# Products and query tiles in column halves, with a new allowance for other work, in a fused long convolution and attention

## The chip, the cores and the metric

The kernel runs on one core of one Trainium2 chip. The metric is the device time of one execution in microseconds (us). All data is float32.

## What is computed

Two independent results stand side by side in the output. The first 576 columns are a long convolution: a kernel `K` of 2048 steps for each of 576 channels, made from a sum of 128 complex exponentials a channel, is convolved with `u`. The other 576 columns are attention with 32 query heads of 18 columns and one shared key and value head, over 2048 positions.

```python
P = jnp.exp(logdA[:, :, None] * l[None, None, :])
K = jnp.einsum("dn,dnl,dn->dl", Cc, P, dB).real
y = irfft2(rfft2(up) * rfft2(Kp))[:L] + u * Dskip

q = (x @ wq).reshape(B, S, H, Dh);  k = x @ wk;  v = x @ wv
p = softmax(einsum("bhqd,bkd->bhqk", q, k) * Dh ** -0.5)
out = einsum("bhqk,bkd->bhqd", p, v).reshape(B, S, H * Dh) @ wo
```

## The kernel before, in words

**The attention rounds.** `main` (line 664) walks over 1024 pairs in a fixed order: 4 chunks of 512 queries, 8 groups of four heads, 16 blocks of 128 keys, 2 pairs of heads. A pair has a score tile of 128 keys by 2 x 512 queries. The pairs are taken in rounds of three (`NS`). In a round TensorE (PE) makes the scores of three pairs (`scores`, line 419), ScalarE (ACT) takes their exponentials from PSUM into an SBUF tile `P` (`exponentials`, line 430), and PE multiplies earlier `P` tiles with V (`product`, line 721). One product covers two pairs, that is four heads: four matmuls in the four 32-column strips of the array, 512 columns wide, into the bank `ops`; it adds up over 16 key blocks. Then VectorE (DVE) copies `ops` out (`gather`, line 440) and the next group of heads may begin. PSUM has three score tiles of two banks, one bank for `ops`, and one bank `f` for all other work. There are eight `P` tiles (`NP`).

**Other work.** Three streams of other work are written as generators that yield before each piece: the query projections and output projections (`side`: `qproj`, line 322; `outproj`, `outproj_part`), the preparation of outputs (`prep`), and the convolution (`conv`). The convolution runs over 12 pieces of 48 channels: tables of exponentials on DVE, kernel tiles on PE (`kgen`), transforms on PE (`transform`, tiles `lu`, `hu`, `lk`, `hk`), products on DVE, inverse transforms on PE (`iy`), and a few long ACT functions (sine, exponential) with table loads. Every PE piece of other work writes the bank `f` and DVE must empty it before the next tile.

**What sets the order.** The instructions of PE, ACT and DVE are emitted in an order written by the program itself. A `Clock` in the program keeps planned times for the three engines (each piece adds a fixed charge: 0.88 a product, 0.465 a query group, 0.485 an output-projection group). Between scores and products, `fill` (line 690) hands out pieces of other work while an allowance (`credit`) or the planned time before the next scores permits it; the constants in lines 37 to 46 set it. `free` (line 765) is the planned time at which all three score buffers are free. Queues are in order: a piece that waits holds up what is behind it on its engine.

**Query tiles.** `qproj` makes a tile of 126 (or 72) rows by 512 queries in ten groups of four matmuls, 256 columns each, into one bank. DVE then makes three passes over all 512 columns from that bank: `qh` (a rounded copy), `ql` (the remainder), `ab` (the largest absolute value); the bank is free after the third. `queries` (line 359) stores `qh` and `ql` to DRAM, makes `aw` and a small bound matmul `up` from `ab`, and `fetch` reads the stored rows back into `aug`, from which the scores are made. `qh` and `ql` have one buffer each. The first query tile (`first_queries`, line 351) uses these two buffers as well.

**The end.** `outproj_part` adds the output projection of the last chunk in parts while the rounds still run; `finish` (line 535) does the parts that are left (`rest`) after the last products, scales the last group and stores.

Of the kernel before, what the change touches and what calls it, by code (L numbers as in the profile page):

```python
# [17 lines left out]
P = 128  # L18
# [17 lines left out]

RATE = 1.75
PACE = 1.68
AHEAD = 0.7
TOTAL = 340.0  # L40
LAST = 500
DEFER = 0.5
NAUG = 5
HEAD = 12

LEFT = 0.85

# [13 lines left out]
class Clock:  # L61
# [6 lines left out]
    def __init__(self):  # L68
        self.t = self.v = self.a = 0.0
        self.work = 0.0  # L70
        self.s = [0.0] * NS
        self.fill = 0.0

    def pe(self, cost, *after):
# [6 lines left out]
    def filled(self):  # L81

        self.fill = self.v + 0.25

    def dve(self, out, rate):
# [35 lines left out]
class Stream:  # L121
# [26 lines left out]
    def go(self, step, credit, lock=None):  # L148

        k = self.k  # L150
        ready = self.ready if self.kind != "p" or self.holds else max(self.ready, k.fill)
        if not self.live or self.kind == "b" or self.kind == "p" and (credit <= 0 or k.t < ready or lock not in (None, self)):
            return False
        if self.kind == "v" and (k.t < self.ready or k.v > k.t + self.ahead):
            return False
        if self.kind == "w":
            if self.asked == step:
                return False
            self.asked = step
        self.advance()  # L160
        return True
# [10 lines left out]
class Attention:  # L172
# [36 lines left out]
    def setup(self, tp, conv):  # L209
# [17 lines left out]

        keys = cp.tile([P, 5, CT], F32R, tag="oT", name="keys")
        kh, kl, self.vt = keys[:, 0, :], keys[:, 1, :], keys[:, 2, :].bitcast(F32)
        self.ident = cp.tile([P, P], F32, name="ident")  # L230
# [91 lines left out]
    def qproj(self, c, m, xt):  # L322

        nc, V, K = self.nc, self.V, self.k
        m0, mn = MT[m]
        self.q_left = 10
        yield "p", K.fill, False
        ps = self.bank(CT, f"q{c}_{m}")
        for f in range(2):
            sl = slice(f * 256, f * 256 + 256)  # L330
            for k in range(5):
                matmul4(nc, ps[:, sl], self.wq[m][:, k, :], xt[:, k, sl], start=(k == 0), stop=(k == 4))
                K.pe(0.465)
                self.q_left -= 1
                self.units += 1
                if (f, k) != (1, 4):
                    yield "p", 0.0, True
        K.v = max(K.v, K.t)
        qh, ql, ab = self.operands(c, m)
# [4 lines left out]
        yield from self.queries(c, m, qh, ql, ab)  # L344

    def operands(self, c, m):
        return (self.p2.tile([P, CT], F32R, tag="qh", name=f"qh{c}_{m}", bufs=1),
                self.p2.tile([P, CT], F32R, tag="ql", name=f"ql{c}_{m}", bufs=1),
                self.p2.tile([P, 2], F32, tag="ab", name=f"ab{c}_{m}"))

    def first_queries(self, ps):
        nc, V, mn = self.nc, self.V, MT[0][1]
        qh, ql, ab = self.operands(0, 0)
        nc.scalar.activation(qh[:mn, :], ps[:mn, :], AF.Copy)
        V.tensor_tensor(ql[:mn, :], ps[:mn, :], qh[:mn, :].bitcast(F32), op=ALU.subtract)
        V.tensor_reduce(ab[:mn, 0:1], ps[:mn, :], axis=AX.X, op=ALU.max, apply_absolute_value=True)
        yield from self.queries(0, 0, qh, ql, ab)

# [125 lines left out]
    def outproj(self, c):  # L484
# [4 lines left out]
        for t in range(4):  # L489
            ob = self.p1.tile([P, D], F32, tag="ob", name=f"ob{c}_{t}")  # L490
            for n in range(2):
                cs = slice(n * 288, (n + 1) * 288)
                ps = self.bank(288, f"op{c}_{t}_{n}")
                for m, (m0, mn) in enumerate(MT):
                    matmul4(nc, ps, o[:mn, m, t * P:(t + 1) * P], self.wo[:mn, m, cs], start=(m == 0), stop=(m == 4))
                    K.pe(0.485)
                    self.o_left -= 1
                    self.units += 1
                    if m < 4:
                        yield "p", 0.0, True  # L500
# [166 lines left out]
    def main(self, conv, flag):  # L667
# [22 lines left out]
        def fill(then):  # L690
# [3 lines left out]
            while more:  # L694
                more = False
                credit = state["credit"] - (K.t - t - idle)
                urgent = self.due < self.step + 8
                late = self.late()
                for st in (prep, side, conv) if urgent else (prep, conv, side):
# [18 lines left out]
            state["filled"] += K.t - t  # L718
            state["credit"] = max(state["credit"] - (K.t - t), -0.8)

        def product(n):
            nonlocal o_ps
            c, g, kb, _ = pairs[2 * n]
            if kb == 0:
                fill(self.o_free)
                o_ps = self.ps_o.tile([P, CT], F32, tag="o", name=f"ops{c}_{g}")
            for j in range(4):
                nc.tensor.matmul(o_ps[32 * j:32 * j + 32, :], self.v[:, kb, :], pts[2 * n + j // 2][:, j % 2, :],  # L728
                                 start=(kb == 0), stop=(kb == 15), tile_position=(0, 32 * j))
            K.pe(0.88, done[2 * n + 1] + 0.1, self.o_free if kb == 0 else 0.0)  # L730
            read[n] = K.t + 0.2
            state["credit"] -= 0.88
            if kb == 15 and (c, g) != (NCH - 1, 7):
# [6 lines left out]
        for r in range(0, len(pairs), NS):  # L740
# [12 lines left out]
            for i in new:  # L753

                while (i - NP) // 2 >= behind:
                    product(behind)
# [5 lines left out]

            state["credit"] = min(state["credit"] + NS / 2 * (0.88 + min(max((TOTAL - state["filled"]) / max(LAST - s, 20), 0.45), 0.7 if s < 384 else 0.9)), 1.2 + 0.88)
# [16 lines left out]
            if kb >= 12 and nxt < 64:  # L780
                force(lambda: nxt in self.ready)
        while behind < len(pairs) // 2:
            product(behind)
# [95 lines left out]
class Conv:  # L879
# [203 lines left out]
    def transform(self, src, y, nm, ready):  # L1083
# [4 lines left out]
        for j in range(2):  # L1088
            for half in (1, 0):
                yield "p", max(ready, K.fill), False  # L1090
                ps = self.bank(2 * NE, f"{'lh'[half]}{nm}{j}").rearrange("p (r n) -> p r n", r=2)
                for r in (2 * half, 2 * half + 1):
                    q = 4 * j + r
                    matmul4(nc, ps[:, r % 2, :], self.dft[:, q * P:(q + 1) * P], src(r))
                    K.pe(0.33)
                    if r % 2 == 0:
                        yield "p", 0.0, True
# [15 lines left out]
    def back(self, k, kt):  # L1113
# [58 lines left out]
        for hf in range(2):  # L1172
# [3 lines left out]
            for r in (2 * hf, 2 * hf + 1):  # L1176
                for j in range(2):
                    q = 8 + 4 * j + r
                    matmul4(nc, ps[:, r % 2, :], self.dft[:, q * P:(q + 1) * P], w[:, 4 * j + r, :], start=(j == 0), stop=(j == 1))
                K.pe(0.65)  # L1180
                if r % 2 == 0:
                    yield "p", 0.0, True
# [158 lines left out]
```

## Time and profile before

| | |
|---|---|
| median of 3 runs | 1245.04 us (1243.87 to 1247.54) |
| profiled execution | 1244.84 us |
| its span, first to last instruction | 1242.8 us |
| mean granted PE clock | 0.983 |
| first and last exponential start | 33.0 and 1220.5 us |
| PE, DVE, ACT busy | 1161.4, 987.5, 1048.6 us |

An engine's busy time counts each moment once in which it has an instruction in work; PE's is no measure of PE at its peak, since matmuls overlap. In a timeline row stand the start, the length, engine, line, operation, the tiles and, behind `x`, how many records were merged; in brackets the idle time before it and what ended it. A float32 matmul leaves two records, so a group of four matmuls is `x8`. PEld is PE's loading of weights, which runs beside PE. The chain of waits goes back from the last instruction to what released each step.

### The profile page before, as it was taken

What the parts mean: (1) busy time and instruction counts of PE and PEld (TensorE: products, weight loads), DVE (VectorE), ACT (ScalarE), POOL (GpSimd) and SP (SyncE); (2) the same over time, 40 slices, a digit from 0 to 9 for tenths busy, and PEclk for the clock granted to TensorE, in tenths of its full rate; (3) what the DMA queues carried; (4) which work ended last, traced back from release to release, by engine and by line L of the source; (5) the groups of instructions that cost most, each with busy time, mean ns of one, the idle gap of its engine ahead of it and who ended that gap; (6) DMA issues with size and microseconds to landing.
All of it is one profiled execution on the core that took longest, in us unless ns stands there. A gap on an engine that the chain in (4) does not pass through costs nothing.

```text
span 1242.8 us, 32583 instructions
## 1 busy us (share of the span) xinstructions
PE 1161.4 (93%) x13786; PEld 478.1 (38%) x13786; DVE 987.5 (79%) x1606; ACT 1048.6 (84%) x1101; POOL 53.6 (4%) x93
## 2 busy tenths in 40 slices
PE   7799999999999899899999899999998989999997
PEld 2344333334334334334334334334433334433433
DVE  4576986996897897796898895798589899799573
ACT  2598979899998888888988888888898988988893
POOL 2010000100000000000000000000000000000000
PEclk8799999999999999999999999999999999999999
DMA  6532222213223112023223002122212211111111
GB/s 228 163 98 80 82 61 67 74 37 111 77 86 106 34 36 83 25 72 103 95 53 116 28 20 72 56 76 79 80 35 62 88 34 63 42 49 61 60 40 41
DMA packets 55051, 89.32 MB, mean 72 GB/s; under 512 B 14173, under 2 KB 24797, under 8 KB 54388
## 3 DMA queue, kind: packets, MB, share of 16 engines
q1 hardware_dynamic: 43911, 72.46, 18.1%
q0 software_dynamic: 10016, 13.98, 4.4%
q8 instruction: 110, 1.80, 0.6%
q10 hardware_dynamic: 972, 0.74, 0.2%
q14 instruction: 42, 0.34, 0.1%
HBM read 49.28 MB, written 36.50 MB: 69 GB/s over the span
## 4 chain that ended last, share of the span: by engine, by line
PE 60%; DVE 27%; ACT 5%; issue 4%; DMA 2%; SPq 1%; ACTq 0%; DVEq 0%
PE ops L728 24%; PE s L426 16%; DVE tab L99 5%; PE op L169 5%; ACT P L437 4%; PE q L169 3%; DVE ks L99 3%; DVE acc L99 3%; PE kg L1051 3%; PE iy L169 2%; DVE pt L99 2%; DVE f L99 2%; DVE r L99 2%; PE lk L169 1%; PE hk L169 1%
## 5 line engine op out<-in xcount | busy, mean ns | idle before, releaser
L437 ACT ACTIVATE P<-s 128x1024 f32<-128x1024 f32 x992 | 937.7, 1031 | 134.6 <-PE s L426 130.2
L728 PE MATMUL ops<-P,v_sb 128*32 128x512 f32 x4096 | 519.7, 600 | 10.9 <-DVE o L103 10.8
L426 PE MATMUL s<-aug,kaug 55*128 55x512 f32 x2048 | 365.3, 443 | 28.8 <-ACT P L437 23.5
L426 PEld LDWEIGHTS s<-aug,kaug 55*128 55x128 f32 x2048 | 170.2, 185 | 343.2 <-ACT P L437 301.1
L728 PEld LDWEIGHTS ops<-P,v_sb 128*32 128x32 f32 x4096 | 115.6, 110 | 159.1 <-issue 115.7
L169 PE MATMUL q<-x,wq_sb 128*32 128x256 f32 (+2 forms) x1480 | 105.9, 397 | 2.7 <-DVE sck L99 1.2
L169 PE MATMUL op<-wo_sb,oT 126*32 126x288 f32 (+1 forms) x1088 | 83.4, 430 | 7.7 <-DVE sck L99 3.7
L169 PEld LDWEIGHTS q<-x,wq_sb 128*32 128x32 f32 (+1 forms) x1480 | 47.4, 110 | 54.3 <-issue 25.6
L99 DVE TENSOR_TENSOR tab<-tab,tt 128x576 f32<-128x576 f32 (+1 forms) x72 | 59.1, 821 | 1.6
L103 DVE COPY ksb<-kg 128x192 f32<-128x192 f32 x48 | 17.5, 364 | 53.7 <-PE kg L1051 53.6
L99 DVE TENSOR_TENSOR tab<-tab 128x576 f32<-128x576 f32 (+1 forms) x72 | 59.0, 819 | 1.1
L99 DVE TENSOR_TENSOR tab<-sum,r 128x576 f32<-128x576 f32 (+1 forms) x72 | 58.9, 818 | 0.0
L99 DVE TENSOR_TENSOR tt<-f,sum 128x576 f32<-128x576 f32 (+1 forms) x72 | 58.9, 817 | 0.0
L99 DVE TENSOR_TENSOR tab<-r,dif 128x576 f32<-128x576 f32 (+1 forms) x72 | 58.8, 816 | 0.0
L169 PEld LDWEIGHTS op<-wo_sb,oT 126*32 126x32 f32 (+1 forms) x1088 | 33.1, 114 | 51.8 <-issue 28.4
L435 ACT ACTIVATE P<-s,nb 128x1024 f32<-128x1024 f32 x32 | 33.1, 1115 | 22.8 <-PE s L426 22.6
L99 DVE TENSOR_TENSOR pt<-us,ks 128x1728 f32<-128x1728 f32 (+2 forms) x36 | 48.6, 1351 | 0.1
L99 DVE TENSOR_TENSOR acc<-acc,pt 128x1728 f32<-128x1728 f32 (+2 forms) x36 | 48.6, 1351 | 0.1
L99 DVE TENSOR_TENSOR sck<-lk,sck 128x384 f32<-128x384 f32 x48 | 24.5, 553 | 28.2 <-PE lk L169 28.2
L1051 PEld LDWEIGHTS kg<-tab 128*32 128x32 f32 x2304 | 36.7, 111 | 24.5 <-issue 8.8
L376 POOL DMA_DIRECT2D qd<-qh x38 | 24.0, 635 | 498.4 <-DVE qh L103 498.4
L1051 PE MATMUL kg<-tab 128*32 128x64 f32 x2304 | 42.4, 223 | 1.9 <-DVE tab L99 1.5
(131 smaller groups left out, 992.9 us busy)
## 6 DMA issues: line engine op xcount, KB each, us to landing
aug<-qd SPq DMA_DIRECT2D x124, 110.0 KB
od<-o SPq DMA_DIRECT2D x31, 256.0 KB
qd<-qh POOLq DMA_DIRECT2D x30, 252.0 KB, 6.0
u<-u SPq DMA_DIRECT2D x12, 384.0 KB
kd<-ksb SPq DMA_DIRECT2D x12, 384.0 KB
kt<-kd SPq DMA_DIRECT2D x48, 96.0 KB
outa<-u SPq DMA_DIRECT2D x12, 384.0 KB
oT<-od SPq DMA_DIRECT2D x16, 252.0 KB
```

What stands on the lines that cost most here:

```text
L99: return self.v.tensor_tensor(out, *a, **k)
L103: return self.v.tensor_copy(out, *a, **k)
L169: nc.tensor.matmul(ps[j:e], w[:, j:e], x, start=start, stop=stop, tile_position=(0, j))
L376: q.dma_start(qd[h0 + n0:h1, row:row + 18, :], src[n0 * DH:mn, :].bitcast(F32))
L426: nc.tensor.matmul(ps[:, j, :], self.kaug[r, kb * P:(kb + 1) * P], t[r, :], start=True, stop=True)
L435: nc.scalar.activation(pt, ps, AF.Exp, scale=SCALE, bias=self.nb)
L437: nc.scalar.activation(pt, ps, AF.Exp, scale=SCALE)
L728: nc.tensor.matmul(o_ps[32 * j:32 * j + 32, :], self.v[:, kb, :], pts[2 * n + j // 2][:, j % 2, :], start=(kb == 0), stop=(kb == 15), tile ...
L1051: nc.tensor.matmul(ps[32 * g:32 * g + 32, d, :], t[:, :32], t[:, 32:], start=(j == 0), stop=(j == 1), tile_position=(0, 32 * g))
```

## The change

- A product is made in two halves of 256 columns, each with its own four matmuls; the unit that the rounds hand out is the half, and a round's due is three halves. A half is charged 0.435 in the clock.
- A query tile is made in two halves of 256 columns, each in a tile of its own in the bank `f`. DVE copies each half and makes its remainder; then the bank counts as free; the maximum is taken from the copy in SBUF, by halves, and a third small reduction joins the two.
- The first query parts stand in two unused slices of the `keys` tile, not in the buffers of `qh` and `ql`.
- `fill` computes its allowance with new constants, and DVE's run ahead of the plan is cut by `NEAR` while a PE piece that needs emptying, or the end of a product sum, is planned soon (`near`, `due`, `last`).

```diff
-RATE = 1.75
-PACE = 1.68
-AHEAD = 0.7
-TOTAL = 340.0
-LAST = 500
-DEFER = 0.5
+RATE = 1.7223
+PACE = 2.6661
+AHEAD = 0.6441
+TOTAL = 238.4006
+LAST = 660.2161
+DEFER = 0.3799
...
+    def near(self):
+        return NEAR if self.t + SOON > min(self.due, self.last) else 0.0
...
-        if self.kind == "v" and (k.t < self.ready or k.v > k.t + self.ahead):
+        if self.kind == "v" and (k.t < self.ready or k.v > k.t + self.ahead - k.near()):
...
+        qh, ql, ab = self.operands(c, m)
         for f in range(2):
             sl = slice(f * 256, f * 256 + 256)
+            yield "p", K.fill, False
+            ps = self.bank(256, f"q{c}_{m}_{f}")
             for k in range(5):
-                matmul4(nc, ps[:, sl], self.wq[m][:, k, :], xt[:, k, sl], start=(k == 0), stop=(k == 4))
+                matmul4(nc, ps, self.wq[m][:, k, :], xt[:, k, sl], start=(k == 0), stop=(k == 4))
...
-        V.tensor_copy(qh[:mn, :], ps[:mn, :])
-        V.tensor_tensor(ql[:mn, :], ps[:mn, :], qh[:mn, :].bitcast(F32), op=ALU.subtract)
-        V.tensor_reduce(ab[:mn, 0:1], ps[:mn, :], axis=AX.X, op=ALU.max, apply_absolute_value=True)
-        K.filled()
+            V.tensor_copy(qh[:mn, sl], ps[:mn, :])
+            V.tensor_tensor(ql[:mn, sl], ps[:mn, :], qh[:mn, sl].bitcast(F32), op=ALU.subtract)
+            K.filled()
+            V.tensor_reduce(ab[:mn, f:f + 1], qh[:mn, sl].bitcast(F32), axis=AX.X, op=ALU.max, apply_absolute_value=True)
+        V.tensor_reduce(ab[:mn, 2:3], ab[:mn, 0:2], axis=AX.X, op=ALU.max)
...
-        qh, ql, ab = self.operands(0, 0)
+        qh, ql, ab = self.keys[:, 3, :], self.keys[:, 4, :], self.p2.tile([P, 3], F32, tag="ab", name="ab0_0")
...
-                    spare = credit - 0.3 if st is not side or urgent or late or side.holds else 0.0
-                    wait = then - K.t - (1.2 if st is side and not urgent and not side.holds and self.units > 0.64 * self.step + HEAD else 0.15)
-                    if st.go(self.step, max(spare, wait, 0.3 * (st is side and side.holds and conv.lags(self.step) and credit > -1.0)), holder()):
+                    spare = credit - LEAST
+                    if st is side and not (urgent or late or side.holds):
+                        spare -= SLOPE * max(ahead, 0.0)
+                    elif st is side and side.holds:
+                        spare += HOLD
+                    wait = then - K.t - (GAP_NEW if st is side and not urgent and not side.holds else GAP)
+                    if st.go(self.step, max(spare, wait), holder()):
...
+            cs = slice(f * 256, f * 256 + 256)
             for j in range(4):
-                nc.tensor.matmul(o_ps[32 * j:32 * j + 32, :], self.v[:, kb, :], pts[2 * n + j // 2][:, j % 2, :],
-                                 start=(kb == 0), stop=(kb == 15), tile_position=(0, 32 * j))
-            K.pe(0.88, done[2 * n + 1] + 0.1, self.o_free if kb == 0 else 0.0)
+                nc.tensor.matmul(o_ps[32 * j:32 * j + 32, cs], self.v[:, kb, :], pts[2 * n + j // 2][:, j % 2, cs],
+                                 start=(kb + f == 0), stop=(kb + f == 16), tile_position=(0, 32 * j))
+            K.pe(0.435, done[2 * n + 1] + 0.1, self.o_free if kb == 0 else 0.0)
+            state["credit"] -= 0.44
...
-            while behind < r // 2:
-                fill(free() - 0.88 * (r // 2 - behind))
-                if behind == r // 2 - 1 and K.t + 0.88 > free() + DEFER:
+            target = min(r - 1, 2 * (r // 2))
+            while behind < target:
+                fill(free() - 0.44 * (target - behind))
+                if behind >= target - 2 and K.t + 0.44 > free() + DEFER:
                     break
                 product(behind)
                 behind += 1
```

More of the change, by code (lines that the diff above doesn't have):

```diff
@@ L34 @@
 NP = 8
-RATE = 1.75
-PACE = 1.68
-AHEAD = 0.7
-TOTAL = 340.0
-LAST = 500
-DEFER = 0.5
-NAUG = 5
-HEAD = 12
-LEFT = 0.85
+RATE = 1.7223
[4 more added lines that the diff above has]
+DEFER = 0.3799
+NAUG = 5
+LEFT = 1.0372
+CAP = 0.5454
+DEBT = 0.8847
+GROUP = 0.2874
+HOLD = 0.3303
+LEAD = 0.8335
+MOST = 0.7745
+LEAST = 0.5036
+NEAR = 0.4134
+SLOPE = 0.2673
+SOON = 0.5397
+URGENT = 7.3595
+GAP = 0.2175
+GAP_NEW = 0.6686
 LATE = {1: [0], 3: [1], 5: [2], 6: [3]}
@@ L72, in __init__ @@
         self.fill = 0.0
+        self.due = self.last = 1e9
+    def near(self):
+        return NEAR if self.t + SOON > min(self.due, self.last) else 0.0
     def pe(self, cost, *after):
@@ L83, in filled @@
         self.fill = self.v + 0.25
+        self.due = 1e9
     def dve(self, out, rate):
@@ L498, in outproj @@
                     self.units += 1
+                    K.due = K.t + 0.465 * (4 - m)
                     if m < 4:
@@ L781, in main @@
                 force(lambda: nxt in self.ready)
-        while behind < len(pairs) // 2:
+        while behind < len(pairs):
             product(behind)
@@ L1095, in transform @@
                     K.pe(0.33)
+                    K.due = K.t
                     if r % 2 == 0:
@@ L1180, in back @@
                 K.pe(0.65)
+                K.due = K.t
                 if r % 2 == 0:
```

33 lines of the change are left out of this document (18 added, 15 removed).

## Prediction

> **What bounds the kernel now.** I read the page first: shares of the engines, the chain of work that ended last, the costliest groups.
>
> ```profile
> span 1242.8 us, 32583 instructions
> PE 1161.4 (93%) x13786; PEld 478.1 (38%) x13786; DVE 987.5 (79%) x1606; ACT 1048.6 (84%) x1101; POOL 53.6 (4%) x93
> PE 60%; DVE 27%; ACT 5%; issue 4%; DMA 2%; SPq 1%; ACTq 0%; DVEq 0%
> L437 ACT ACTIVATE P<-s 128x1024 f32<-128x1024 f32 x992 | 937.7, 1031 | 134.6 <-PE s L426 130.2
> ```
>
> No engine is full. ACT must run 1048.6 us and stands idle 134.6 us before exponentials, nearly all of it waiting for PE's scores; PE holds 60% of the chain. So the time is made where PE and ACT miss each other. The program runs in rounds: PE makes scores for three pairs, then products with V and other work, and ACT takes the three exponentials. Next I read the timelines of PE and ACT, first where PE is late:
>
> ```profile
> 1203.97 0.96 PE L426 MATMUL s<-aug,kaug 55*128 55x512 f32 x6
> 1204.87 1.51 PE L169 MATMUL iy<-w,dft_sb 128*32 128x192 f32 x32
> 1206.19 1.04 PE L728 MATMUL ops<-P,v_sb 128*32 128x512 f32 x8
> 1207.16 0.96 PE L426 MATMUL s<-aug,kaug 55*128 55x512 f32 x6
> 1208.06 0.69 PE L169 MATMUL op<-wo_sb,oT 126*32 126x288 f32 x8
> 1208.57 1.90 PE L728 MATMUL ops<-P,v_sb 128*32 128x512 f32 x16
> 1210.40 0.96 PE L426 MATMUL s<-aug,kaug 55*128 55x512 f32 x6
> 1211.00 2.85 ACT L437 ACTIVATE P<-s 128x1024 f32<-128x1024 f32 x3 [0.38 <-PE s L426]
> ```
>
> Durations of rows overlap, so I price by starts and by differences. One product (x8) shows 1.04, two (x16) 1.90: 0.86 each. Four inverse-transform groups take 1206.19 - 1204.87 = 1.32, 0.33 each; an output-projection group 0.51, about 0.48 without the change of shape. The round from 1207.16 to 1210.40 lasts 3.24 and holds 0.48 + 1.72 = 2.20 of work: 1.04 goes to scores and switching. The round before lasts 3.19 with 1.32 + 0.86 = 2.18: 1.01. So a PE-bound round lasts its other work L plus about 1.03, and ACT idles (0.38 here). Then where PE is early:
>
> ```profile
> 251.93 0.91 PE L426 MATMUL s<-aug,kaug 55*128 55x512 f32 x4
> 253.25 0.50 PE L426 MATMUL s<-aug,kaug 55*128 55x512 f32 x2 [0.41 <-ACT P L437]
> 253.68 1.92 PE L728 MATMUL ops<-P,v_sb 128*32 128x512 f32 x16
> 255.53 0.97 PE L426 MATMUL s<-aug,kaug 55*128 55x512 f32 x6
> 256.51 1.04 PE L728 MATMUL ops<-P,v_sb 128*32 128x512 f32 x8
> 249.41 6.53 ACT L437 ACTIVATE P<-s 128x1024 f32<-128x1024 f32 x7
> 256.13 5.61 ACT L437 ACTIVATE P<-s 128x1024 f32<-128x1024 f32 x6 [0.19 <-PE s L426]
> ```
>
> Seven exponentials take 6.53: 0.933 each, 2.80 a round. That is the floor. Below L = 2.80 - 1.03 = 1.77 PE waits for ACT to free a score buffer (0.41 idle at 253.25), and that time is not given back in a later, heavier round, since there are only three score buffers. And even these plain rounds, one product and two in turn, lose 0.19 of ACT a pair: two whole products are too much for one round, one is too little.
>
> **The change part by part.**
>
> *Halves.* Each product becomes two of 256 columns: 4096 more matmul records and weight loads. Before has no such product, but query projection is the same shape (128 rows, 32 columns, 256 wide):
>
> ```profile
> 58.63 1.93 PE L169 MATMUL q<-x,wq_sb 128*32 128x256 f32 x32
> 62.25 1.50 PE L169 MATMUL q<-x,wq_sb 128*32 128x256 f32 x24
> 254.13 0.13 PEld L728 LDWEIGHTS ops<-P,v_sb 128*32 128x32 f32 x4 [0.30 <-issue]
> ```
>
> Eight records more cost 0.43, so two halves cost 0.86, as one product does. I take 0; what hides the doubled loads (0.13 for four) is that they run beside the matmuls, as they do in the query rows. Bounds: 0, and 0.13 on each of 1024 more groups of four, 133 us, if that cover were gone; the nearest row says 0. The Trainium skill, "TensorE: Matmul & The Clock Gate", section "Back-to-back issue gap", gives each warm matmul a fixed 2.5 ns beyond its columns; 1024 more groups of four would be an estimated 2.6 us, and the sum that much later. These rows cannot resolve that.
>
> *Evenness.* I took the order of PE's instructions in both built programs, split it at the scores into rounds, and added up each round's L (product 0.86, half 0.43, query group 0.43, output-projection group 0.48, transform group 0.32, half a convolution-kernel tile 0.67, the program's own charge). Leaving out the first six rounds and those with the long convolution's functions on ACT, before has 293 rounds with mean L 1.99, after 290 with the same mean, but the spread falls from 0.54 to 0.27: the commonest rounds of after are one piece of other work and three halves, L about 1.94, 2.97 us. Shortfalls below 1.77: before, 26 rounds near 0.87 (23.4 us), 19 near 1.43 (6.4), 57 near 1.72 (3.0), in all 32.8; after, 1 round at 0.92 (0.9), 21 near 1.35 (8.8), 13 near 1.70 (0.9), in all 10.5. Gain **22**. It is counted once, as ACT time that PE no longer has to catch up.
>
> *Plain pairs.* 25 rounds before hold one product alone, beside rounds with two; 0.19 each pair is 5 us. Three halves are L = 1.29 and fit under 1.77. Gain **5**.
>
> *Rounds with ACT's long functions.* There are 11 such stretches in both.
>
> ```profile
> 209.56 2.85 ACT L437 ACTIVATE P<-s 128x1024 f32<-128x1024 f32 x3 [0.54 <-PE s L426]
> 212.28 1.26 ACT L977 ACTIVATE m<-m 128x1248 f32<-128x1248 f32 x1
> 218.63 2.86 ACT L437 ACTIVATE P<-s 128x1024 f32<-128x1024 f32 x3
> ```
>
> From 212.28 to 218.63 ACT works without a gap; it sets their length. L in the 33 rounds concerned is 93 us before, 90 after. I take 0; bounds -5 and +5.
>
> *Start.* The first query parts get space of their own.
>
> ```profile
> 35.44 4.50 PE L169 MATMUL q<-x,wq_sb 128*32 128x256 f32 x40 [0.55 <-DVE v_sb L103]
> 46.23 1.35 PE L426 MATMUL s<-aug,kaug 55*128 55x512 f32 x6
> 54.10 0.30 PE L169 MATMUL up<-sel_sb,aw 126*32 126x8 f32 x8 [6.53 <-DVE aw L107]
> 49.57 0.69 DVE L103 CAST qh<-q 126x512 fp32r<-126x512 f32 x1 [6.65 <-DMA qd<-qh]
> 58.33 3.12 ACT L435 ACTIVATE P<-s,nb 128x1024 f32<-128x1024 f32 x3 [8.30 <-PE s L426]
> ```
>
> DVE waited 6.65 us for the stores that still read the one query buffer; behind it stood the small bound matmul at 54.10, behind that on PE the products and the next scores, and ACT idled 8.30. In after that copy waits for PE alone. 8.3 go. One of the five query groups that stood before the second scores at the slow start moves behind them: 4.50/5 = 0.9. What is late next: the query rows of the second head group, fetched after the bound; that chain starts earlier, its user some 9 us earlier too, so up to 5 us may come back. Gain **9**, bounds 4 and 10.
>
> *Query tiles in halves.* 19 tiles: three DVE passes of 512 columns become six of 256 and a short one.
>
> ```profile
> L99 DVE TENSOR_TENSOR ql<-q,qh 126x512 fp32r<-126x512 f32 x16 | 11.1, 691 | 2.6 <-DMA qd<-ql 2.2
> L111 DVE TENSOR_REDUCE ab<-q 126x1 f32<-126x512 f32 x16 | 10.9, 680 | 0.0
> L562 DVE TENSOR_TENSOR o_last<-o_last,bc 128x256 f32<-128x256 f32 x2 | 0.8, 420 | 2.2 <-PE bc L582 1.2 <-PE bc L576 1.0
> L111 DVE TENSOR_REDUCE un<-up 128x1 f32<-128x8 f32 x20 | 3.2, 158 | 0.4 <-PE up L169 0.4
> ```
>
> 0.69 + 0.69 + 0.68 = 2.06 a tile becomes 6 x 0.42 + 0.16 = 2.68: 12 us more on DVE. DVE's share of the chain is 27%: loss **3** (bounds 0 and 12). Against it PE's one spare bank is free after two short passes, 0.84 instead of 2.06, since the maximum is now read from the copy; the DMAs stay as many.
>
> *Left for the end.* By the order, 8 output-projection groups more stand after the last products, and the last four inverse-transform groups and two halves more stand between the last scores and the end.
>
> ```profile
> 1219.91 0.51 PE L426 MATMUL s<-aug,kaug 55*128 55x512 f32 x2
> 1222.76 2.91 PE fin L169 x48
> 1226.30 4.99 PE fin L169 x80
> ```
>
> The tail is PE's (the two rows of the chain). 8 x 0.48 = 3.9; and 1.3 + 6 x 0.43 = 3.9 in place of 0.48 + 1.72 = 2.2 gives 1.7: loss **5.5**. The rounds have that work less, L in all 706 for 709: gain **3**, since most of them are PE-bound.
>
> *The new allowance* has no price of its own: it acts by the order, which is counted above. The rule that holds DVE back when a bank is due can only change waits for DVE; I take 0 (see rivals).
>
> Sum on the profiled execution, 1244.84 (span 1242.8 and 2.0 around it; the median 1245.04 is 0.2 more): -22 - 5 - 9 + 3 + 5.5 - 3 = -30.5, **1214**.
>
> **Rivals.**
>
> *More.* The 293 ordinary rounds of before last 957 us by the starts of their exponentials (the group quoted first), 918 by the rule: 5 of the 39 are the plain pairs, the rest stalls behind DVE such as
>
> ```profile
> 164.10 3.25 PE L728 MATMUL ops<-P,v_sb 128*32 128x512 f32 x16 [2.61 <-DVE o L103]
> 654.22 0.91 PE L1051 MATMUL kg<-tab 128*32 128x64 f32 x48 [0.57 <-DVE tab L99]
> 214.80 0.86 PE L169 MATMUL lk<-kt,dft_sb 128*32 128x192 f32 x16 [0.68 <-DVE sck L103]
> ```
>
> The first stands behind a query tile's three passes. With shorter passes, and DVE held back near a due bank, 20 of the 34 might go: 1194.
>
> *DVE late: slower.* PE runs in order, and in after 243 of 341 rounds open with other work right behind the scores, 203 before. If DVE isn't done there, products and the next scores stand behind. DVE has 12 us more to do in a loop 35 us shorter. Were every third of the 243 to wait 0.57 as at 654.22, 81 x 0.57 = 46 us and 1260; from 54 such waits on it is slower than before. Against it: such waits are few in this trace.
>
> *Loads not hidden: slower.* If a half's weight loads stood before its matmuls, 30 ns on each of the 1024 more groups of four would take the whole gain, the full 0.13 would give 1214 + 133 = 1347. The query rows speak against it. The Trainium skill's page of the same title, section "Part 3: Packing small matmuls", lets a load overlap matmuls only when the row group differs; these have the same rows. By that rule query projection would show it too, and the trace disagrees: 0.43 for eight records.
>
> *Nothing.* If the convolution's dependent chain (DVE 27%) sets the pace, the light rounds were light because nothing was ready; evenness gives nothing, DVE's 3 and the tail's 5.5 stay, and with the start's 9 it is 1244.
>
> **How the numbers follow.** Forecast (1203 to 1225) 0.50; more (below 1203) 0.18; half of it eaten by DVE (1225 to 1241) 0.15; nothing 0.05; DVE late 0.09; loads 0.03. The range leaves out the best few and the slow ones: 1190 to 1240. A measurement here tells about 0.3%, 3.7 us, from no change: faster 0.83, same 0.05, slower 0.12.
>
> **What would show it.** Right: exponentials without the 8.30 gap near 58; half products at 0.43 by starts; ACT's idle before exponentials down from 134.6 to near 105; most rounds near 3.0; the final groups 5 us longer. Wrong: PE idle at L169 or L1051 matmuls behind DVE summing to tens of us (DVE late); halves at 0.5 or more (loads); ACT's idle unchanged outside the start (nothing).

## The result, and the profile after

The changed kernel took 1229.54 us in the median (1226.65 to 1230.26, 4 runs), the one before 1245.24 us (1243.87 to 1247.54, 4 runs, beside it): a ratio of 0.987, 95% interval 0.985 to 0.989. It is 15.7 us faster; 30.5 were forecast. The profiled execution took 1230.26 us.

First the page of the changed kernel: span, busy times, shares of the chain of waits, costliest groups.

```profile
span 1228.0 us, 40862 instructions
PE 1154.1 (94%) x17882; PEld 609.0 (50%) x17882; DVE 994.9 (81%) x1674; ACT 1053.9 (86%) x1101; POOL 53.7 (4%) x93
PE 66%; DVE 23%; DMA 4%; issue 3%; ACT 3%; SPq 0%; DVEq 0%; ACTq 0%
L457 ACT ACTIVATE P<-s 128x1024 f32<-128x1024 f32 x992 | 942.4, 1028 | 118.1 <-PE s L446 111.4
L755 PEld LDWEIGHTS ops<-P,v_sb 128*32 128x32 f32 x8192 | 255.9, 110 | 181.0 <-issue 35.0
```

Weight loads of the product have doubled to 8192, and the span fell all the same. ACT's idle time before exponentials fell from 134.6 to 118.1, where 105 was expected: a little over half of it came. DVE has 7.4 us more to do.

To see where, I cut each profiled span at the starts of the exponentials, in every kernel in the same way: up to the first; the first six rounds; the 33 rounds of the 11 stretches in which ACT runs the convolution's sines (the round in which a sine starts and the two behind it); the other 302 rounds; from the last exponential's start on. Expectations below call the parts start, long functions, ordinary rounds (the 302 without the 7 to 13 that hold another exponential of the convolution or follow one) and tail.

| us of the profiled span | ahead | first 6 | 302 others | 33 at sines | tail |
|---|---|---|---|---|---|
| before | 33.0 | 32.2 | 990.3 | 165.1 | 22.3 |
| after | 32.8 | 22.7 | 968.3 | 176.0 | 28.2 |
| forecast of the difference | 0 | -9 | -27 | 0 | +5.5 |
| difference | -0.2 | -9.5 | -22.0 | **+10.9** | +5.9 |

The sum of the differences, -14.9, is that of the spans (1228.0 - 1242.8 = -14.8) up to rounding. Start and tail came as forecast, the 302 rounds 5 us short; the stretches at the sines, costed at nothing, took 11 back. The 10.9 depends on the cut: with the round ahead of each sine taken in as well (44 rounds), where the changed kernel is shorter, the difference is 6.9.

Here is the worst kind of such a stretch: PE, then DVE, then ACT, from the timelines of the changed kernel.

```profile
131.01 2.35 PE L186 MATMUL q<-x,wq_sb 128*32 128x256 f32 x30 [0.51 <-DVE un L128]
135.98 3.20 PE L186 MATMUL q<-x,wq_sb 128*32 128x256 f32 x21 [2.62 <-DVE ql L116]
...
126.94 1.95 DVE L116 TENSOR_TENSOR pt<-us,ks 128x1728 f32<-128x1728 f32 x1
128.92 1.96 DVE L116 TENSOR_TENSOR acc<-acc,pt 128x1728 f32<-128x1728 f32 x1
130.80 0.16 DVE L128 TENSOR_REDUCE un<-up 128x1 f32<-128x8 f32 x1
...
131.53 1.34 DVE L116 TENSOR_TENSOR pt<-us,ks 128x1152 f32<-128x1152 f32 x1
132.90 1.36 DVE L116 TENSOR_TENSOR acc<-acc,pt 128x1152 f32<-128x1152 f32 x1
134.29 0.76 DVE L116 TENSOR_TENSOR pt<-us,ks 128x576 f32<-128x576 f32 x1
134.97 0.41 DVE L120 CAST qh<-q 72x256 fp32r<-72x256 f32 x1
135.41 0.42 DVE L116 TENSOR_TENSOR ql<-q,qh 72x256 fp32r<-72x256 f32 x1
...
135.04 2.86 ACT L457 ACTIVATE P<-s 128x1024 f32<-128x1024 f32 x3
141.34 3.77 ACT L457 ACTIVATE P<-s 128x1024 f32<-128x1024 f32 x4 [3.44 <-PE s L446]
```

PE has the first query half done by 133.36 (131.01 + 2.35). DVE has a row of convolution passes ahead of it and reaches the copy `qh` at 134.97; PE's second half needs the bank `f` and starts at 135.98, after a wait of 2.62. Behind it in PE's queue stand products and the next scores, and ACT, whose own long functions end at 135, has scores for one round only and then idles 3.44. Five of the 11 stretches hold parts of two halves right behind each other, and four of these lose 2.8 to 4.7 us beyond ACT's own work (nine exponentials at 0.933 and the long functions); in all eleven the loss is 22.2 us, 10.0 in the kernel before. The fifth waits 2.40 and loses 0.7. The list of PE's waits shows the second halves as one row, the first here; the second row is the longest of the others behind DVE (us in total, times, longest):

```profile
PE q L186 <- DVE ql L116: 14.6, 6, 3.0
PE ops L755 <- DVE o L120: 7.7, 12, 1.5
```

### The profile page after: what moved, and what is told of

Its sections match the earlier page's. It is cut to its first block, busy times and chain, and to the rows that moved or that the text cites. A ratio compares the mean times of both kernels' runs of the same rounds, so it can differ in the third digit from the quotient of the medians.

```text
span 1228.0 us, 40862 instructions
## 1 busy us (share of the span) xinstructions
PE 1154.1 (94%) x17882; PEld 609.0 (50%) x17882; DVE 994.9 (81%) x1674; ACT 1053.9 (86%) x1101; POOL 53.7 (4%) x93
## 4 chain that ended last, share of the span: by engine, by line
PE 66%; DVE 23%; DMA 4%; issue 3%; ACT 3%; SPq 0%; DVEq 0%; ACTq 0%
PE ops L755 25%; PE s L446 18%; PE op L186 5%; PE q L186 4%; DVE ks L116 3%; PE iy L186 3%; PE kg L1082 3%; DVE tab L116 3%; DVE acc L116 2%; ACT P L457 2%; DVE f L116 1%; PE lk L186 1%; PE hu L186 1%; PE hk L186 1%; PE fin L186 1%
## 5 line engine op out<-in xcount | busy, mean ns | idle before, releaser
L457 ACT ACTIVATE P<-s 128x1024 f32<-128x1024 f32 x992 | 942.4, 1028 | 118.1 <-PE s L446 111.4
L755 PE MATMUL ops<-P,v_sb 128*32 128x256 f32 x8192 | 533.2, 382 | 7.9 <-DVE o L120 7.7
L446 PE MATMUL s<-aug,kaug 55*128 55x512 f32 x2048 | 350.9, 439 | 10.8 <-ACT P L457 5.7
L755 PEld LDWEIGHTS ops<-P,v_sb 128*32 128x32 f32 x8192 | 255.9, 110 | 181.0 <-issue 35.0
L186 PE MATMUL q<-x,wq_sb 128*32 128x256 f32 (+2 forms) x1480 | 116.2, 413 | 21.8 <-DVE ql L116 14.6
L186 PEld LDWEIGHTS q<-x,wq_sb 128*32 128x32 f32 (+2 forms) x1480 | 48.8, 113 | 71.0 <-issue 40.0
L186 PE MATMUL op<-wo_sb,oT 126*32 126x288 f32 (+1 forms) x1024 | 76.7, 415 | 5.1 <-DVE scu L116 2.5
L186 PEld LDWEIGHTS op<-wo_sb,oT 126*32 126x32 f32 (+1 forms) x1024 | 28.9, 110 | 38.7 <-issue 16.9
L116 DVE TENSOR_TENSOR sck<-lk,sck 128x384 f32<-128x384 f32 x48 | 24.5, 551 | 27.8 <-PE lk L186 27.8
```

The source lines that it names most:

```text
L116: return self.v.tensor_tensor(out, *a, **k)
L186: nc.tensor.matmul(ps[j:e], w[:, j:e], x, start=start, stop=stop, tile_position=(0, j))
L446: nc.tensor.matmul(ps[:, j, :], self.kaug[r, kb * P:(kb + 1) * P], t[r, :], start=True, stop=True)
L457: nc.scalar.activation(pt, ps, AF.Exp, scale=SCALE)
L755: nc.tensor.matmul(o_ps[32 * j:32 * j + 32, cs], self.v[:, kb, :], pts[2 * n + j // 2][:, j % 2, cs], start=(kb + f == 0), stop=(kb + f == ...
```

## The experiments

Two theories at first. **A**: the loss is that of the second query half in the stretches; move it and the gain comes. **B**: the gain was smaller than the rule says, and DVE's lateness shows wherever the order puts it. Each time is a median beside the kernel before on the same chip (1245.2 to 1245.9 there). This is the same cut of every profiled execution:

| us | median | ratio (95%) | ahead | first 6 | 302 others | 33 at sines | tail | half clock |
|---|---|---|---|---|---|---|---|---|
| e1_next_round | 1229.80 | .985-.989 | 31.2 | 22.6 | 970.5 | 175.5 | 27.8 | 6.8, 20.5 |
| e2_query_whole | 1243.26 | .997-.999 | 31.3 | 28.6 | 979.6 | 169.6 | 32.5 | 20.5, 17.1 |
| e3_start_only | 1247.42 | 1.000-1.003 | 32.9 | 34.9 | 991.8 | 163.8 | 22.0 | 6.8, 6.8 |
| e4_product_halves | 1252.08 | 1.004-1.007 | 31.2 | 32.4 | 998.3 | 173.7 | 17.9 | 23.8, 17.2 |
| e5_whole_after | 1256.22 | 1.006-1.010 | 30.8 | 21.6 | 980.4 | 166.5 | 55.2 | 10.2, 20.5 |
| e6_old_start | 1236.28 | .992-.995 | 31.1 | 33.5 | 967.9 | 172.2 | 27.8 | 3.4, 10.2 |
| e7_light_after | 1217.41 | .975-.979 | 31.3 | 22.5 | 968.8 | 164.7 | 27.9 | 6.8, 6.8 |
| e8_light_before | 1237.77 | .992-.995 | 33.4 | 31.9 | 981.5 | 168.1 | 22.1 | 0.0, 20.5 |
| e9_whole_rate | 1264.79 | 1.014-1.018 | 31.5 | 22.8 | 986.6 | 174.2 | 47.3 | 13.7, 23.9 |
| e10_no_hold | 1245.92 | .999-1.002 | 31.4 | 21.7 | 978.6 | 176.0 | 38.1 | 20.8, 26.9 |
| e11_rate | 1239.73 | .994-.997 | 31.4 | 22.6 | 965.5 | 171.7 | 46.5 | 1.0, 12.7 |
| e12_light_more | 1214.98 | .974-.978 | 32.7 | 22.1 | 960.8 | 164.7 | 27.8 | 0.0, 6.8 |

The part ahead of the first exponential, which the edits hardly touch, lies between 30.8 and 33.4: differences of two us in one column mean nothing.

The last column is the time for which PE's granted clock was 0.5, in the 302 and in the 33 rounds; it falls to 0.5 in steps of some 3.4 us and is 1.0 otherwise. In the kernel before it is 6.8 and 10.2, in the changed kernel 3.4 and 20.5. One such step follows the wait in the stretch shown above. Here are the work from there on and the same query half in e7_light_after (below), where PE waits 1.14; the clock stands ahead of the DMA share:

```profile
core 0: us, PE busy (x) PEld busy (x) DVE busy (x) ACT busy (x) POOL busy (x), PEclk, DMA share, GB/s
135.98:139.30 3.32, 3.32 (x26) 1.68 (x29) 3.29 (x5) 1.92 (x3) 0.00 (x0) 0.50 0.00 0
132.59:136.00 3.41, 3.41 (x50) 2.24 (x52) 3.38 (x5) 3.40 (x4) 0.00 (x0) 1.00 0.03 7
```

The 21 records of that half last 3.20 at 0.50 and 1.71 at 1.00. A step therefore costs PE up to 1.7 us on top of the wait ahead of it (half of 3.4, an estimate). All edits but those of e3, e6, e7, e8 and e12 also change the order of PE's work, so a single such run doesn't part the edit from the order that came with it.

**e1_next_round**: the changed kernel, the second query half at the earliest two rounds on.

```diff
         for f in range(2):
             sl = slice(f * 256, f * 256 + 256)
+            for _ in range(2 * f):
+                yield "w", 0.0, False
             yield "p", K.fill, False
```

> After with one thing changed: the second half of a query tile may not be handed out in the same round as the first. Theory A (in the stretches with ACT's long functions the second half waits for DVE to empty the one spare bank, and the scores stand behind it): by the order no such stretch holds both halves of a tile any more, so the stretches lose about 10 us beyond ACT's own work instead of 22, and the time falls by 12 to 15 us to about 1216. Rival B (the stretches cost the same in any order; what was gained or lost is the accident of one order): within 5 us of after, 1225 to 1234. Rival C (DVE is what sets the pace): unchanged, since DVE's work is the same.

1229.8: nothing gained, and theory A falls in this form. The pairs of halves are gone from the stretches, but the order changed with them. The loss beyond ACT's own work fell from 22.2 to 17.9 only: three stretches lose 3.3 to 3.8 each, now behind the convolution's passes `sck` and `scu` or behind `un`. The sum stays at 175.5, since these rounds hold 3.8 us more of ACT's long functions, and the 302 others are no shorter without them.

**e2_query_whole**: the changed kernel with each query tile whole in one bank, DVE's three passes at its end as before.

```diff
+        yield "p", K.fill, False
+        ps = self.bank(CT, f"q{c}_{m}")
         for f in range(2):
-            yield "p", K.fill, False
-            ps = self.bank(256, f"q{c}_{m}_{f}")
...
+        V.tensor_copy(qh[:mn, :], ps[:mn, :])
+        V.tensor_tensor(ql[:mn, :], ps[:mn, :], qh[:mn, :].bitcast(F32), op=ALU.subtract)
+        V.tensor_reduce(ab[:mn, 0:1], ps[:mn, :], axis=AX.X, op=ALU.max, apply_absolute_value=True)
+        K.filled()
```

> After with query tiles made whole in one bank as before (three DVE passes over 512 columns); product halves, allowance and the first query parts' own space stay. Theory A: no wait inside a tile, so the stretches with ACT's long functions lose about 10 us instead of 22; but by the order the rounds are less even (shortfalls 19 instead of 11 us), so about 1219. Rival B: 1225 to 1234. If instead the shorter hold of the spare bank is what carries the gain: slower than after, above 1234.

1243.3: the third answer. The stretches do lose less (169.6 for 176.0), but the start, the tail and the 302 rounds give back more. In the order that this version gets, whole tiles cost 13.7, where the forecast had the halves as a cost of 3. In the 302 rounds 17 us more stand at half clock, an estimated 8.5 of the 11.3 lost there.

**e3_start_only**: the kernel before, with own space for the first query parts and nothing else.

```diff
-        qh, ql, ab = self.operands(0, 0)
+        qh, ql, ab = self.keys[:, 3, :], self.keys[:, 4, :], self.p2.tile([P, 2], F32, tag="ab", name="ab0_0")
```

> Before with only the first query parts in space of their own. By the prediction's step 8.3 us of ACT's idle time goes and nothing else moves: about 1237. Rival: the rows of the second head group are fetched no earlier and the time comes back there: 1241 to 1245.

1247.4: no gain. The wait that goes uncovers another, one round later:

```profile
57.83 0.42 DVE L107 TENSOR_SCALAR sh<-u 8x512 fp32r<-8x512 f32 x1 [9.85 <-DMA qd<-sh]
58.55 3.64 PE L169 MATMUL q<-x,wq_sb 128*32 128x256 f32 x32 [8.18 <-DMA wq_sb<-wq]
64.63 2.12 ACT L436 ACTIVATE P<-s,nb 128x1024 f32<-128x1024 f32 x2 [11.69 <-PE s L427]
```

The third tile's weights have not landed, and DVE waits for the store of the first `sh`. **e6_old_start** asks the reverse: the changed kernel with only that edit undone, the order of PE the same.

```diff
-        qh, ql, ab = self.keys[:, 3, :], self.keys[:, 4, :], self.p2.tile([P, 3], F32, tag="ab", name="ab0_0")
+        qh, ql, ab = self.operands(0, 0)
```

> The changed kernel, but the first query parts back in the one buffer of each kind that all query tiles share; the order of PE's instructions is the same. If their own space is needed, the copy of the second tile's first half waits for the stores again, some 6 us, and ACT with it: 1236 to 1239. If the spreading of the second tile over the first rounds is enough by itself, the copy comes when the stores are done: 1229 to 1231.

1236.3: 6.7 slower than the changed kernel; the first six rounds last 33.5 for 22.7, of which the stretches give some back. The waits of the kernel before return, on DVE, PE and ACT:

```profile
47.87 0.42 DVE L120 CAST qh<-q 126x256 fp32r<-126x256 f32 x1 [8.14 <-DMA qd<-qh]
51.31 1.93 PE L186 MATMUL q<-x,wq_sb 128*32 128x256 f32 x16 [9.04 <-DVE ql L116]
55.38 11.37 ACT L455 ACTIVATE P<-s,nb 128x1024 f32<-128x1024 f32 x11 [11.29 <-PE s L446]
```

So own space is needed and isn't enough. In the changed kernel the second tile is spread over the first rounds, and the third begins when its weights are there:

```profile
50.30 0.23 PE L186 MATMUL up<-sel_sb,aw 126*32 126x8 f32 x8
53.93 0.61 PE L186 MATMUL q<-x,wq_sb 128*32 128x256 f32 x8
52.58 0.41 DVE L124 TENSOR_SCALAR sh<-u 8x512 fp32r<-8x512 f32 x1 [0.35 <-DMA qd<-sh]
```

**e4_product_halves**: the kernel before, with product halves, three a round, under the old allowance.

```diff
+            cs = slice(f * 256, f * 256 + 256)
...
-            K.pe(0.88, done[2 * n + 1] + 0.1, self.o_free if kb == 0 else 0.0)
+            K.pe(0.435, done[2 * n + 1] + 0.1, self.o_free if kb == 0 else 0.0)
+            state["credit"] -= 0.44
...
-            while behind < r // 2:
+            target = min(r - 1, 2 * (r // 2))
+            while behind < target:
```

> Before with only the products in halves, three halves a round; old allowance, whole query tiles, old start. By the prediction's rule for evenness: shortfalls by the order 27 instead of 33 us, 10 us of other work moved out of the tail, so about 1238. If halves by themselves carry the gain of the loop: near 1222. If the doubled weight loads cost 30 ns a group: above 1255.

1252.1, between the expectations: the halves alone lose. The rule for a round gave the ordinary rounds 923.4 in 295 for 918.5 in 293, no gain, and they lasted 970.8 for 957.0. The 33 rounds are 8.6 longer too, without a query half in any. In all 24 us more stand at half clock, an estimated 12 of the 16.6 lost in the two groups of rounds. Now the reverse, **e5_whole_after**: the changed kernel with whole products.

```diff
-            K.pe(0.435, done[2 * n + 1] + 0.1, self.o_free if kb == 0 else 0.0)
-            state["credit"] -= 0.44
+            K.pe(0.87, done[2 * n + 1] + 0.1, self.o_free if kb == 0 else 0.0)
+            state["credit"] -= 0.88
...
-            target = min(r - 1, 2 * (r // 2))
-            while behind < target:
-                fill(free() - 0.44 * (target - behind))
+            while behind < r // 2:
+                fill(free() - 0.88 * (r // 2 - behind))
```

> The changed kernel, but its products with V whole again, one or two a round; query halves, allowance and own space for the first query parts stay. If the even rounds that three half products allow carry the gain, the rule for a round says 5.4 us more in the ordinary rounds (891.9 in 291 rounds for 886.5 in 290) and the lone products beside pairs cost some 5 again: 1240. If the query halves with the new allowance carry it, and product halves give as little here as they did alone on the kernel before: 1226 to 1234.

1256.2, slower than either expectation: the tail alone is 27 us longer. In the 302 rounds it is 12 slower than the changed kernel, at the sines 9.5 faster. **e9_whole_rate** was to take the tail out of it (whole products as in e5_whole_after, and):

```diff
-RATE = 1.7223
+RATE = 1.8
```

> The changed kernel with whole products as in e5_whole_after, and RATE 1.8 for 1.7223, so that the convolution may run further ahead and is not left for the end, which cost e5_whole_after some 27 us in its tail. If product halves matter by the plan that they allow, its ordinary rounds stay as slow as those of e5_whole_after (940 for 924) and the tail is near that of the changed kernel (28): 1238 to 1246. If e5_whole_after was slow by its tail alone: 1226 to 1233.

1264.8: a miss of both. The tail is still 47 us; the 302 rounds are 18 slower than in the changed kernel. So under the new allowance whole products lose 12 and 18 in these rounds, in the two orders tried (the rule gave 5.4 for the first, the lone products 5 more); half clock is an estimated 3 and 5 of that. Under the old allowance the halves gained nothing.

**e7_light_after** and **e8_light_before** ask what DVE's lateness costs, with the order of every instruction kept. 72 passes (block products of the convolution and their sums) do half of their elements, so that part of the convolution is left out; the plan is charged as if they were whole.

```diff
-                tt(t, blk(us, 0, 4 - m), kb, op=ALU.mult)
+                n = shp[1] // 2
+                K.dve(t, 1.04e-3)
+                nc.vector.tensor_tensor(t[:, :n], blk(us, 0, 4 - m)[:, :n], kb[:, :n], op=ALU.mult)
                 yield "v", 0.0, False
-                tt(blk(acc, m, 4), blk(acc, m, 4), t, op=ALU.add)
+                a2 = blk(acc, m, 4)
+                K.dve(a2, 1.04e-3)
+                nc.vector.tensor_tensor(a2[:, :n], a2[:, :n], t[:, :n], op=ALU.add)
```

> The changed kernel with its order on PE, DVE and ACT unchanged, but 72 of DVE's passes (block products of the convolution and their sums) do half of their elements, which leaves out that part of the convolution: about 48 us of DVE's 995. If the part of the forecast that did not come is lost in waits for DVE, the rest above the rule in ordinary rounds (37 us) and the loss at the long functions (22 us) fall by a third or more: 1205 to 1218. If it is lost between PE and ACT themselves (scores, score buffers), nothing moves: 1227 to 1232.

> The kernel before with the same 72 passes halved, order unchanged. If both kernels lose the same to a late DVE, it gains what the changed kernel gains from the same cut (20 or so: 1225), and the change is then worth the same 16. If the changed kernel loses more to DVE than the one before, this one gains less, and the difference between the two light kernels comes near the forecast's 30.

1217.4: 12.1 faster than the changed kernel, and the place is as clear as the size: the 33 rounds at the sines fall from 176.0 to 164.7, as short as before the change; the 302 others, the start and the tail do not move. The same stretch as above, PE and ACT in e7_light_after:

```profile
132.59 1.71 PE L186 MATMUL q<-x,wq_sb 128*32 128x256 f32 x21 [1.14 <-DVE ql L116]
...
133.71 5.60 ACT L457 ACTIVATE P<-s 128x1024 f32<-128x1024 f32 x6
139.50 1.02 ACT L457 ACTIVATE P<-s 128x1024 f32<-128x1024 f32 x1 [0.19 <-PE s L446]
```

2.62 became 1.14, and ACT's 3.44 became 0.19. The four stretches that lost most behind a second half, 14.5 in all, now lose 2.0. Their waits are shorter by 5.8 together (2.62, 2.95, 2.83 and 2.62 became 1.14, 1.08, 1.94 and 1.10), and the step at half clock that followed each of them is gone, an estimated 6.8 more: 12.6 for the 12.5 measured. The fifth is the control: its wait stays (2.40 and 2.42), a step now follows it, and its loss rises by 1.7. So the loss is the wait for DVE and, about as much again, the half clock behind it.

The kernel before gained 7.5 from the same cut, in its 302 rounds, not at the sines. With DVE light the change is worth 20.4 (1237.8 - 1217.4) instead of 15.7.

**e12_light_more**: the same, and three of the five passes that make each table on half of their elements as well (left out too), order kept.

```diff
-            tt(im, im, re, op=ALU.add)
+            h = n // 2
+            V.v.tensor_tensor(im[:, :h], im[:, :h], re[:, :h], op=ALU.add)
...
-            tt(t, L(f), H(sm), op=ALU.mult)
+            V.v.tensor_tensor(t[:, :h], L(f)[:, :h], H(sm)[:, :h], op=ALU.mult)
...
-            tt(re, re, t, op=ALU.subtract)
+            V.v.tensor_tensor(re[:, :h], re[:, :h], t[:, :h], op=ALU.subtract)
```

> e7_light_after with 216 more of DVE's passes (three of the five that make each convolution table) on half of their elements as well, order unchanged: some 88 us of DVE's time less again. If what is left above the rule (37.6 us in ordinary rounds, 10.9 at the long functions) is also DVE's: 1195 to 1208. If that remainder is PE against ACT (three score buffers, the switch between kinds of work): 1213 to 1219.

```profile
PE 1145.1 (95%) x17882; PEld 608.4 (50%) x17882; DVE 883.0 (73%) x1674; ACT 1053.5 (87%) x1101; POOL 53.7 (4%) x93
L457 ACT ACTIVATE P<-s 128x1024 f32<-128x1024 f32 x992 | 941.9, 1028 | 99.8 <-PE s L446 92.6
```

1215.0: 70 us less of DVE's work (953.1 in e7_light_after) buy 2.4 in the median (the profiled execution, 1210.26, is the fastest of five). The stretches stay at 164.7. What is left above the rule is hardly DVE's total load.

**e10_no_hold** is the changed kernel in which DVE is no longer held back ahead of a due bank or of the last product of a group, **e11_rate** the changed kernel with nothing but another order. Each has one line of its own:

```diff
-NEAR = 0.4134
+NEAR = 0.0
```

```diff
-RATE = 1.7223
+RATE = 1.74
```

> The changed kernel without the rule that holds DVE back when a bank or the last product of a group is due (NEAR 0). The forecast cost that rule at nothing. The order changes too: by the rule for a round its ordinary rounds are as long (899.0 in 294 for 886.5 in 290, 3.06 each), and one of the 11 stretches of long functions instead of five has parts of two query halves right behind each other. If two halves in a stretch are the only cause of the loss there: 1217 to 1223. If the loss goes to other places when the order changes, as with e1_next_round, or the hold is worth something: 1226 to 1236.

> The changed kernel with RATE 1.74 for 1.7223: nothing but the order of other work changes, the rule for a round gives 885.5 for 886.5. It shows how far the time moves with the order alone. If the order's even rounds set the time: 1227 to 1232. If the places where DVE is late decide, it can lie 3 to 8 us off on either side.

1245.9 misses both expectations, 1239.7 lies past the far end of the second. Without the hold the 302 rounds take 10 us more, an estimated 8.7 of it by 17 us more at half clock; its 33 rounds stay at 176.0, though only one stretch has two query halves behind each other, so there other pieces wait for DVE. With another order alone the 302 rounds take 3 less. And the tails are 10 and 18 us longer, which I had not foreseen. PE at the end of e11_rate, and DVE:

```profile
1194.58 0.67 PE L186 MATMUL op<-wo_sb,oT 126*32 126x288 f32 x8
1207.88 1.19 PE L186 MATMUL op<-wo_sb,oT 126*32 126x288 f32 x8 [12.63 <-DVE part L120]
1209.65 1.19 PE L186 MATMUL op<-wo_sb,oT 126*32 126x288 f32 x8 [0.58 <-DVE part L120]
1211.42 1.19 PE L186 MATMUL op<-wo_sb,oT 126*32 126x288 f32 x8 [0.58 <-DVE part L120]
...
1199.64 0.69 DVE L116 TENSOR_TENSOR oT<-oT,db 126x512 f32<-126x512 f32 x1 [5.32 <-DMA db<-rden]
1206.77 0.69 DVE L116 TENSOR_TENSOR oT<-oT,db 126x512 f32<-126x512 f32 x1 [5.33 <-DMA db<-rden]
1207.38 0.45 DVE L120 COPY part<-op 128x288 f32<-128x288 f32 x1
```

Four output-projection groups are left behind the last product. The copy that empties their bank stands on DVE behind two scalings that wait for a DMA, 5.3 us each; from 1198.3 to 1215.4 PE's granted clock is 0.50. In the changed kernel none is left there, and PE goes straight on:

```profile
1201.01 2.77 PE L755 MATMUL ops<-P,v_sb 128*32 128x256 f32 x48
1203.60 3.10 PE L186 MATMUL fin<-wo_sb,oT 126*32 126x288 f32 x48
```

The same wait stands in the tails of e5_whole_after (10.14), e9_whole_rate (12.22) and e10_no_hold (6.88). Without its longer tail e11_rate would lie near 1221 (1239.7 - 18.3); such a version was not run.

## Why the prediction was half right

The result lies where the forecast had *half of it eaten by DVE* (1225 to 1241, chance 0.15). That is what happened, though not in the rounds in which the forecast looked for it.

**Halves at no price: right.** In the last fence six halves run from 1201.01 to 1203.60, 0.432 each; 0.43 was forecast. The rival of loads that are not hidden is out: 8192 loads of 0.110 lie beside the matmuls. The rule of the Trainium skill ("TensorE: Matmul & The Clock Gate", section "Part 3: Packing small matmuls") that a load overlaps only for another row group is not what these rows show, as the prediction read from the query rows; its other rule, 2.5 ns a matmul, an estimated 2.6 us here if the four strips of a group run side by side, cannot be told apart in them.

**Evenness, plain pairs, moved work: right in kind, 5 short.** -22.0 came for -27. The rule's own difference came whole: the ordinary rounds fell from 957.0 (293) to 923.6 (290), 33.4, where the rule gave 918.5 to 886.5, 32.0. What stands above the rule hardly changed, 38.5 before and 37.1 after; the 5 of the plain pairs were to come out of it, so that term is mis-sized. The excess has moved: the commonest rounds, L near 1.93, were put at 2.97, and over a hundred of them in the trace of after have a median of 3.02 and a mean of 3.09. In e7_light_after and e12_light_more the median is 3.02 again, so it isn't DVE's load. That the third score waits for a buffer would explain it, but that was only argued. The forecast also took evenness as a property of the halves. e4, e5 and e9 suggest that it belongs to halves and allowance together; each of them has another order too.

**Start: right in size, the mechanism too simple.** -9.5 for -9. The step "what is late next" named the second head group's rows; e3 shows that the third tile's weights and the `sh` store were late next and cost the whole gain. It came because the second tile is also spread over the first rounds: with own space and whole tiles (e2) the first six rounds last 28.6, with halves 22.7.

**Query halves, +3: wrong in sign as far as one order can tell.** DVE's busy time rose by 7.4, where 12 was put. In e2 taking the halves back costs 13.7 and doesn't gain 3; but e2 has another order, and e11 shows that an order alone can cost 10, so the size is not shown.

**ACT's long functions, 0 with bounds of 5: the step that failed.** It took 10.9. The reasoning was that ACT sets the length of these stretches and that L in them is as large as before. L was as large (90 us for 93, by the order), and with the same order e7 needs 164.7 for 165.1; what was left out is that PE waits for DVE in the middle of a stretch when a second piece needs the single bank `f`, since DVE is loaded with convolution passes just there, and that PE then works on at half clock. The rival *DVE late* named the first half of this, but spread it over all rounds that open with other work and priced a wait at 0.57; here five waits of 2.4 to 3.0, four of them followed by a step at half clock, did it. e7 shows that this is the loss: the same order, less DVE work, and 11.3 us are back, in these rounds and no others, split about evenly between the waits and the clock. It is not a property of query halves: in e1, e4 and e10 few or no such pairs stand in the stretches, and these are as long, behind other pieces.

**The allowance, 0: not nothing.** e10 and e11 change only it and lose 16 and 10. The hold on DVE is worth about 10 in the 302 rounds (one order tried; most of it goes with the half clock), and whether output-projection groups are left behind the last product is worth 10 to 20. The forecast took the order from the built program and so had this in its tail: +5.9 for +5.5.

What stays open is most of the rest above the rule, some 30 us in the ordinary rounds even with a light DVE (916.1 in e12_light_more for 886.5 by the rule); no step at half clock falls into its 302 rounds, so it isn't that either.

## What to carry to other kernels

A sum of PE work by rounds says what an even order can give; what it gives is decided where a queue in order meets a buffer that exists once, so go through the stretches in which another engine is loaded and ask of each second use of that buffer who empties it, and what stands ahead of that on its engine. An edit that removes a wait should be tried alone and taken out alone: here own space and product halves gave nothing or less when put alone into the kernel before, and cost 7 us and 27 or more, most of it in the tail, when taken out of the changed one. To learn what a late engine costs, make its work lighter and keep the order; an edit that changes the order moves the waits and shows only their sum. And read the granted clock beside the waits: a long wait is priced too low by its length alone.

## What the runs showed of the hardware

Waits of PE can be followed by half clock. After the second halves' waits of 2.62 to 2.95 us in the changed kernel the granted clock was 0.5 for some 3.4 us, four times out of four; after those of 1.08 to 1.94 in e7_light_after it stayed at 1.0; after the fifth, 2.40 and 2.42, it was once 1.0 and once 0.5. Shorter waits close together can do the same: in the kernel before a step begins at 801.7, behind waits of 0.68 and 1.23 within three us. What decides between these was not tested.

A chain through PE, the single bank and DVE with nothing beside it costs far more than its parts among other work: in the tail of e11_rate output-projection groups follow each other at 1.77 us (1207.88, 1209.65, 1211.42 above), while one among other work adds 0.48. Part of this is the clock, 0.50 there: the row of a group is 1.19 long, 0.67 at 1194.58 ahead of the drop. The stores and reloads of scale factors through DRAM make DVE wait 5.3 us each. The other surprise is how little must change: RATE by 1%, with the same work in total, moved the time by 10 us, 18 more in the tail and 8 less ahead of it.
